# Chunk attention and a MISH feed-forward on one core: order of sums' parts, divisions ahead of conversions, weights kept from slot 4, k loaded apart, last weight sum in another buffer

## The chip, the cores and the metric

The kernel runs on one core of a Trainium2 chip. The metric is the time of one execution on the device in microseconds; the median of several runs is compared. The engines are named as in the profile: PE multiplies matrices, DVE, ACT and POOL work elementwise, SP issues nearly all transfers, which 16 DMA engines carry out.

## The reference

Attention inside chunks of 64 tokens gives 4608 tokens of 512 values; a feed-forward with the MISH function follows. All is float32.

```python
scores = scale * np.matmul(q_c, k_c.transpose(0, 1, 2, 4, 3))      # chunks of 64 x 64
scores = scores - np.max(scores, axis=-1, keepdims=True)
attn = np.exp(scores)
attn = attn / (np.sum(attn, axis=-1, keepdims=True) + 1e-09)
x = np.matmul(attn, v_c)                                           # 4608 x 512 after reordering
h = x @ w_in                                                       # 512 x 2048
sp = np.where(h > 20.0, h, np.log1p(np.exp(np.minimum(h, 20.0))))
out = (h * np.tanh(sp)) @ w_out                                    # 2048 x 512
```

## The kernel before

**Split operands.** PE multiplies in a short float format, so every float32 operand is kept as a high part (a conversion, on ACT) and a low part (operand minus high part, on DVE or POOL), and each product is three matmuls: low by high, high by high, high by low. Names with `_hi` and `_lo` make these parts.

**Order.** The whole program is written in the order in which it is to be issued (`manual_schedule`); each engine takes its own instructions in that order. SP issues transfers in order too, at most 8 of them in flight. Buffers are handed round: "turns" are rings of pieces in one tile (`st_turns`: four of 4 KB in "sums"), `Free` is a list that gives out the place that has been free longest, and the pool `at` has three 8 KB buffers for q, k, v and the like.

**Slots.** The first two blocks of 512 tokens are multiplied plainly, in 32 slots s = 0 to 31, one for each of 2 blocks and 16 slices f of the hidden width. Slot s does the up matmuls of slice s+1 (`up`, 12 matmuls into `h`), MISH and the split of its result into `g` (`g_hi`, `g_lo`), and the down matmuls of slice s-1 (`down`, 12 matmuls into `o_o`). In the first 16 slots the weights also come in: `w_load` (512 KB on SP), `w_scale` (ACT), `w_bits` (DVE), `w_hi` (ACT), `w_lo` (DVE). `keep_weights(f)` writes the split pieces that the later sets need to the chip's memory (`dwi`, `dwo`): four transfers of 256 KB for even f, two for odd f, in slot f + KEEP. The JOBS (`t_sum`, `t_diff`, `t_hi`, `t_lo`) make sums of weights and write them there too; the last one, `LAST_JOB`, is done in sets 0 and 1.

**Attention.** It is done in pairs of tiles (a pair is 256 tokens): load q and k, scores, maximum, subtract, exponential, sum and inverse (`a_inverse`), division (`a_norm`, on DVE), transposes through PE and a copy back, values. Four pairs ("quick", j = 4 to 7) are spread over slots 13 to 29: their scores fall in slots 14, 18, 22, 26, their divisions and transposes in 16, 20, 24, 28. Ten more pairs are planned in the sets by `plan_pair(j, then)`, where `then` is the step of the exponential; `on_pe` places a pair's matmuls.

**Sets.** The other 28 tiles go through a scheme of seven products for four, in sets z of 14 steps, 84 matmuls each in the steady part. Even steps hold a group of up matmuls (`s_up`, into `al`, `b` or `g`), odd steps a group of down matmuls (`s_down`, into `d`) that belongs to earlier sets. `plan_set` places the work of a set: copies of partial results out of PE's banks (`s_copy`: "p1", "u2", "p5"), additions (`s_c`), MISH (`s_mish`), sums of results ("T1" to "T4", `s_t`), and the two parts of each operand of the down matmuls (`s_hi`, `s_lo`; POOL does the low parts of 22, T2 and T3 and the sums T2 and T3). `s_out` adds `d` to "sums" on DVE, or copies it there on ACT the first time. `ring_load` and `wo_load` bring the weights of the sets back (1 MB and 512 KB each). Two slots' down matmuls and the last stores (`store`) fall into the first sets; `when(z, step, ...)` adds work to a step.

Of the kernel before, what the change touches and what calls it, by code (L numbers as in the profile page):

```python
# [18 lines left out]
P = 128  # L19
# [6 lines left out]
def kernel(  # L26
# [196 lines left out]
    def w(step, n):  # L223
        if n < len(order):
            steps[step](*order[n])
# [6 lines left out]
    def load_qk(j, qk=None, ts=(BOTH,), queues=(nc.sync, nc.sync)):  # L232
        if qk is None:
            qk = [at.tile([P, 2, H, CHUNK], F32, name=f"{n}_{j}", tag="A") for n in "qk"]
        for t in ts:
            for x, src, queue in zip(qk, (q, k), queues):
                queue.dma_start(
                    out=x[:, t], in_=src[2 * j : 2 * j + 2][t].rearrange("t p h c -> p t h c")
                )
        st[j] = {"q": qk[0], "k": qk[1]}  # L240
# [64 lines left out]
    def a_inverse(j, t=BOTH):  # L305
        p = st[j]["p"][:, t].rearrange("p t g c k -> p (t g) c k")
        r = small(j, "r", t)
        nc.vector.tensor_reduce(out=r.rearrange("p c n -> p n c"), in_=p, op=ALU.add, axis=AX.X)  # L308
        nc.vector.tensor_scalar(out=r, in0=r, scalar1=1e-9, scalar2=None, op0=ALU.add)
        nc.vector.reciprocal(out=r, in_=r)  # L310

    def a_norm(j, t=BOTH, engine=nc.vector):
        p = st[j]["p"][:, t].rearrange("p t g c k -> p c (t g) k")
        r = st[j]["r", t.start]
        engine.tensor_tensor(
            out=p, in0=p, in1=r.unsqueeze(3).broadcast_to([P, 2, r.shape[2], CHUNK]), op=ALU.mult
        )
# [297 lines left out]
    def t_hi(m, s):  # L615
        d = tw[m, s]
        for i in range(2):
            if (m, s) == LAST_JOB:
                d["s", i] = at.tile([P, 2, 2, 2 * P], F32R, name=f"s_last{i}", tag="A")
            else:  # L620
                d["s", i] = st_turns.next([2, 2, 2 * P], F32R)
            nc.scalar.copy(out=d["s", i][:, :, 0], in_=d["t", i])

    def t_lo(m, s):
# [173 lines left out]
    def s_up(z, i):  # L798
# [26 lines left out]
        [("xo", 49 * KB + i * UNIT) for i in range(4)]  # L825
        + [("u", i * UNIT) for i in range(9)]
        + [("yr", i * UNIT) for i in range(4)]
        + [("g", i * UNIT) for i in range(4)]
        + [("u", i * UNIT) for i in range(9, 18)]
    )  # L830

    def x1_open():
# [160 lines left out]
        JOBS[NF - 2 + n] = ("io"[n % 2], n // 2)  # L993

    N = NB * NF
    KEEP = 11

    def slot(s):
        a = plan.get(s, {})
        e = quick.get(s, {})  # L1000
        n = 2 * s + 3
        behind = JOBS.get(s - 1)

        if 1 <= s and s + 1 < N:
            up(s + 1, last="w")
        if "v" in e:
            a_values(e["v"])
        if a.get("t", 0) > PAIRS:
            a_transpose(a["t"])
        if "v" in a:  # L1010
            a_values(a["v"])
        if 1 <= s < N - 1:
            down(s - 1)
        if a.get("t", 0) == PAIRS:
            a_transpose(PAIRS)
        if "s" in a:
            a_scores(a["s"])
        if "s" in e:
            a_scores(e["s"])

        if NF <= s < N:
            g_hi(s)
            g_lo(s)
        if a.get("load", 0) > PAIRS:
            load_qk(a["load"])
        if "load" in e and s != NF + 1:
            load_qk(e["load"])
        w("load", n + 4)
        w("hi", n)
        w("scale", n + 2)  # L1030
        w("bits", n + 1)
        w("lo", n)
        if "max" in a:
            a_max(a["max"])
        if "max" in e:
            a_max(e["max"])
            a_sub(e["max"])
            load_v(e["max"])
        if "norm" in e:
            a_inverse(e["norm"])  # L1040
            a_norm(e["norm"])
            a_transpose(e["norm"])
        if a.get("norm", 0) > PAIRS:
            a_norm(a["norm"])
        if plan.get(s - 1, {}).get("norm", 0) == PAIRS:
            a_norm(PAIRS)
        if a.get("t", 0) > PAIRS:
            a_copy(a["t"])
        if "exp" in a:
            a_exp(a["exp"])  # L1050
        w("load", n + 5)
        if "x" in a:
            a_hi(a["x"])
        if s < NF:
            g_hi(s)
            g_lo(s)
        if s + 1 < N:
            mish(s + 1)
        if "max" in e:
            a_exp(e["max"])  # L1060
        w("hi", n + 1)
        w("scale", n + 3)
        w("bits", n + 2)
        w("lo", n + 1)
        if "max" in a:
            a_sub(a["max"])
        if a.get("exp", 0) > PAIRS:
            a_inverse(a["exp"])
        if a.get("norm", 0) == PAIRS:
            a_inverse(PAIRS)  # L1070
        if a.get("t", 0) == PAIRS:
            a_copy(PAIRS)
        if "x" in a:
            a_lo(a["x"])
        if "v" in e:
            a_x(e["v"], 0)
            a_x(e["v"], 1)
        if "norm" in e:
            a_copy(e["norm"])
        if "max" in a:  # L1080
            load_v(a["max"])
        if 0 <= s - KEEP < NF:
            keep_weights(s - KEEP)
        if behind:
            t_hi(*behind)
        if s in JOBS:
            t_sum(*JOBS[s])
        if behind:
            t_lo(*behind)
        if s in JOBS:  # L1090
            t_diff(*JOBS[s])
        if s == NF:
            load_qk(quick[s + 1]["load"])
        if s == NF:
            x_open()
        if s >= 1 and s % NF == 0:
            store(s // NF - 1)
# [3 lines left out]
    def when(z, i, *ops):  # L1101
        due.setdefault((z, i), []).extend(ops)
# [4 lines left out]
    def plan_set(z):  # L1107

        b, s = divmod(z, NS)

        def at_(m, *ops):
            when(*divmod(STEPS * z + m, STEPS), *ops)

        at_(0, lambda: s_copy(z, "p1", ("a", z)))
        at_(2, lambda: s_c(z, 11), lambda: s_mish(z, 11))
        at_(3, lambda: s_hi(z, 11))
        at_(4, lambda: s_copy(z, "u2", ("a", z)))
        at_(5, lambda: s_raw(z), lambda: s_lo(z, 11))
        at_(6, lambda: s_copy(z, "p5", "g"))
        at_(8, lambda: s_c(z, 22), lambda: s_mish(z, 22))  # L1120
        at_(9, lambda: s_hi(z, 22))
        at_(10, lambda: s_c(z, 12), lambda: s_mish(z, 12), lambda: s_lo(z, 22))
        at_(11, lambda: s_t(z, "T1"), lambda: s_t(z, "T3"))
        at_(12, lambda: s_mish(z, 21), lambda: s_hi(z, 21), lambda: s_hi(z, "T1"), lambda: s_hi(z, "T3"))
        at_(13, lambda: s_t(z, "T2"), lambda: s_lo(z, 21), lambda: s_lo(z, "T1"), lambda: s_lo(z, "T3"))
        at_(15, lambda: s_t(z, "T4"), lambda: s_hi(z, "T2"), lambda: s_lo(z, "T2"))
        at_(17, lambda: s_hi(z, "T4"), lambda: s_lo(z, "T4"))
        if s == NS - 1 and b + 1 < NSB:
            plan_x(z, b + 1)

# [11 lines left out]
    def plan_pair(j, then):  # L1142

        start = then - 5

        def at_(n, *ops):
            when(*divmod(n, STEPS), *ops)

        def on_pe(n, op):
            pe.setdefault(divmod(n, STEPS), []).append(op)  # L1150

        at_(start - 7, lambda: p_load(j))
        on_pe(start, lambda: p_scores(j))
        at_(then + 4, lambda: load_v(j))
        for t in range(2):
            at_(start + 1 + 2 * t, lambda t=t: p_max(j, t))
            at_(start + 2 + 2 * t, lambda t=t: p_sub(j, t))
            at_(then, lambda t=t: p_exp(j, t))
            at_(then + 3 + t, lambda t=t: p_sum(j, t))
            at_(then + 6 + 2 * t, lambda t=t: p_norm(j, t))  # L1160
            at_(then + 11, lambda t=t: p_copy(j, t))
            at_(then + 15, lambda t=t: a_x(j, t))
        on_pe(then + 10, lambda: p_transpose(j))
        on_pe(then + 14, lambda: p_values(j))

    ZN = NSB * NS
# [19 lines left out]
    with tc.manual_schedule():  # L1186
# [23 lines left out]
            when(0, i + 1, lambda m=m: x_lo(0, m))  # L1210
        for at_step, i, ts in (
            ((0, 1), N - 2, (0, 1)),
            ((0, 5), N - 2, (2, 3)),
            ((0, 9), N - 1, (0, 1)),
            ((1, 3), N - 1, (2, 3)),
        ):
            pe[at_step] = [lambda i=i, ts=ts: down(i, ts)]
            if i == N - 1:
                when(*at_step, lambda ts=ts: store(NB - 1, ts))
        when(0, 11, *(lambda n=n: wo_load(n) for n in range(4)))  # L1220
        slot(N - 1)
        y_open()
        banks_a.close()
# [2 lines left out]
            places[n] = ps_b.tile([P, DM], F32, name=n, tag=n)  # L1226
        for j, then in zip(range(AHEAD[-1] + 1, NPAIR), EXPS):
            plan_pair(j, then)
        for m, step in (5, t_sum), (6, t_diff), (22, t_hi), (25, t_lo):
            when(*divmod(m, STEPS), lambda step=step: step(*LAST_JOB))  # L1230
        for z in 2, 17:
            when(z, 2, x_late)
# [51 lines left out]
```

## Time and profile before

| | |
|---|---|
| median of 3 runs | 820.83 us (820.49 to 822.52) |
| profiled execution | 819.81 us, its span 818.0 us |
| busy: PE / DVE / ACT / POOL | 98% / 73% / 60% / 34% of the span |
| DMA | 202.33 MB, mean 247 GB/s |
| chain that ended last | PE 75%, DVE 11%, DMA 5%, ACT 5% |

The span is what the profiler saw of the instructions; the execution's time has some 1.8 us around it. Matmuls overlap, so a busy PE isn't a PE at its peak. In rows of a timeline the first number is the start, the second how long the group took; a bracket gives the engine's idle time just before and what ended it. The slots run to 218.5 us, the sets from there.

### The profile page before, as it was taken

The page shows a single profiled execution, that of the slowest core. Times are in us where ns is not written, and L with a number is a line of the kernel's source. Part 1 is how long each engine was busy: PE and PEld are TensorE (multiplying, and loading weights), DVE is VectorE, ACT ScalarE, POOL GpSimd, SP SyncE. Part 2 cuts the span into 40 slices and gives each one's busy share as a digit, 9 for nine tenths or more (in the row PEclk, how much of TensorE's full clock was granted, in tenths as well). Part 3 has the DMA queues.
Part 4 walks back from the last instruction along what each step waited for, and adds up shares of the span by engine and source line. Part 5 has one row for each costly group of instructions (what it writes and reads, how often), then busy time and mean ns, then how long its engine had stood idle before and what let it go on. Part 6 is the DMA issues. An engine that isn't in the chain of part 4 may idle for free.

```text
span 818.0 us, 15365 instructions
## 1 busy us (share of the span) xinstructions
PE 799.5 (98%) x5974; PEld 706.9 (86%) x5974; DVE 593.2 (73%) x929; ACT 489.2 (60%) x867; POOL 274.9 (34%) x239
## 2 busy tenths in 40 slices
PE   8999999999999999999999999999999999999996
PEld 7778887778888998888899999889999999999996
DVE  6898887778865586799657668986575888455566
ACT  5988864655667564665666556557564564644440
POOL 2100025556354332432233235333232444323340
PEclk9999999999999999999999999999999999999999
DMA  8756778999787876576986666788766667866547
GB/s 309 236 177 231 211 257 279 356 369 353 262 301 290 284 245 201 197 266 228 299 302 231 223 206 222 247 293 268 258 232 206 206 206 244 280 220 220 182 129 167
DMA packets 84553, 202.33 MB, mean 247 GB/s; under 512 B 13569, under 2 KB 36609, under 8 KB 77313
## 3 DMA queue, kind: packets, MB, share of 16 engines
q1 hardware_dynamic: 80480, 199.91, 72.7%
q10 hardware_dynamic: 4000, 1.44, 0.8%
q8 instruction: 47, 0.77, 0.4%
q14 instruction: 26, 0.20, 0.1%
HBM read 162.53 MB, written 38.80 MB: 246 GB/s over the span
## 4 chain that ended last, share of the span: by engine, by line
PE 75%; DVE 11%; DMA 5%; ACT 5%; issue 2%; SPq 1%; POOL 0%; ACTq 0%; POOLq 0%
PE d L927 30%; PE al L809 17%; PE g L809 9%; PE o_o L416 5%; PE h L381 4%; PE b L809 4%; PE av L255 2%; PE s L255 2%; DMA k<-in_k 1%; DVE sums L955 1%; DMA dwi<-sums 1%; DVE sums L958 1%; DMA ring<-dwi 1%; PE pt L719 1%; DVE r L308 1%
## 5 line engine op out<-in xcount | busy, mean ns | idle before, releaser
L927 PE MATMUL d<-u,wo 128*128 128x448 f32 x800 | 207.3, 367 | 1.2 <-DVE u L887 0.9
L955 DVE TENSOR_TENSOR sums<-d,sums 128x448 f32<-128x448 f32 x192 | 119.3, 621 | 96.1 <-PE d L927 95.2
L809 PE MATMUL al<-xo,ring 128*128 128x448 f32 x768 | 177.3, 367 | 0.8 <-ACT y L853 0.8
L927 PEld LDWEIGHTS d<-u,wo 128*128 128x128 f32 x800 | 149.5, 188 | 14.5 <-DVE sums L955 1.4
L809 PEld LDWEIGHTS al<-xo,ring 128*128 128x128 f32 x768 | 143.4, 188 | 13.9 <-ACT y L853 2.0
L809 PE MATMUL g<-xo,ring 128*128 128x448 f32 x384 | 88.7, 366 | 0.0
L809 PEld LDWEIGHTS g<-xo,ring 128*128 128x128 f32 x384 | 71.7, 188 | 5.8
L927 PE MATMUL d<-g,wo 128*128 128x448 f32 x194 | 57.2, 365 | 0.0
L927 PE MATMUL d<-yr,wo 128*128 128x448 f32 x184 | 56.2, 369 | 0.0
L877 ACT ACTIVATE y<-y 128x448 f32<-128x448 f32 x26 | 15.0, 578 | 62.6 <-DVE y L863 62.6
L877 ACT ACTIVATE b<-b 128x448 f32<-128x448 f32 x32 | 16.9, 529 | 59.4 <-DVE b L863 59.3
L927 PE MATMUL d<-xo,wo 128*128 128x448 f32 x166 | 51.3, 368 | 0.0
L887 POOL TENSOR_TENSOR u<-y,u 128x448 fp32r<-128x448 f32 x20 | 24.3, 1216 | 78.4 <-ACT u L881 78.4
L909 POOL TENSOR_TENSOR z<-y,z 128x448 f32<-128x448 f32 x27 | 32.7, 1210 | 44.3 <-DVE y L909 36.7
L809 PE MATMUL b<-xo,ring 128*128 128x448 f32 x192 | 44.7, 368 | 0.0
L610 POOL TENSOR_TENSOR c<-c 128x256 f32<-128x256 f32 x12 | 10.3, 865 | 97.9 <-DVE c L578 96.0
L887 POOL TENSOR_TENSOR g<-y,yr 128x448 fp32r<-128x448 f32 x10 | 11.6, 1158 | 94.0 <-ACT yr L881 94.0
L381 PE MATMUL h<-x,xo 128*128 128x512 f32 x168 | 41.2, 394 | 0.0
L416 PE MATMUL o_o<-xo,g 128*128 128x512 f32 x168 | 41.0, 393 | 0.0
L927 PEld LDWEIGHTS d<-g,wo 128*128 128x128 f32 x194 | 36.4, 188 | 2.9
L809 PEld LDWEIGHTS b<-xo,ring 128*128 128x128 f32 x192 | 35.7, 188 | 3.1
L927 PEld LDWEIGHTS d<-yr,wo 128*128 128x128 f32 x184 | 34.5, 188 | 3.7 <-DVE sums L955 0.6
(226 smaller groups left out, 1633.6 us busy)
## 6 DMA issues: line engine op xcount, KB each, us to landing
ring<-dwi SPq DMA_DIRECT2D x56, 1024.0 KB, 7.1
wo<-dwo SPq DMA_DIRECT2D x112, 512.0 KB, 3.9
sums<-in_w_in SPq DMA_DIRECT2D x16, 512.0 KB, 4.6
sums<-in_w_out SPq DMA_DIRECT2D x16, 512.0 KB, 4.1
q<-in_q SPq DMA_DIRECT2D x16, 512.0 KB, 7.0
k<-in_k SPq DMA_DIRECT2D x16, 512.0 KB, 6.9
v<-in_v SPq DMA_DIRECT2D x16, 512.0 KB, 6.5
dwo<-sums SPq DMA_DIRECT2D x14, 512.0 KB, 5.6
```

Of the source, the lines that this page charges most:

```text
L255: nc.tensor.matmul(o[h * CHUNK : (h + 1) * CHUNK, c, t - ts.start, g], lhsT=l[rows, t, 2 * g + h], rhs=r[rows, t, 2 * g + h], start=True, ...
L308: nc.vector.tensor_reduce(out=r.rearrange("p c n -> p n c"), in_=p, op=ALU.add, axis=AX.X)
L381: nc.tensor.matmul(h[:, cols], lhsT=wi(f, w_, kt), rhs=x[:, kt, cols], start=(n == 0), stop=(n == 3 * NK - 1),)
L416: nc.tensor.matmul(acc[t], lhsT=g[:, sl], rhs=w_part(f, w_), start=(f == 0 and n == 0), stop=(f == NF - 1 and n == 2),)
L610: nc.gpsimd.tensor_tensor(out=o, in0=a, in1=b, op=op)
L719: nc.tensor.transpose(out=d["pt"][:, t, g], in_=d["p", t][:, g].rearrange("p c k -> p (c k)"), identity=ident,)
L809: nc.tensor.matmul(o[:, :HALF], lhsT=w_[:, wn, kt * P : (kt + 1) * P], rhs=x[:, xn, kt], start=(n == 0 and k < 3), stop=(n == 5), skip_gro ...
L877: nc.scalar.activation(out=take(z, 12) if n == 12 else i, in_=i, func=AF.Mish)
L887: engine.tensor_tensor(out=u[1][1], in0=source(z, n), in1=raw(u[0][1]), op=ALU.subtract)
L909: engine.tensor_tensor(out=o, in0=l, in1=r, op=ALU.subtract)
L927: nc.tensor.matmul(o[:, :HALF], lhsT=wos[(len(DOWN) * y + kk) % 4][:, i, part, h * P : (h + 1) * P], rhs=x, start=(m == 0 and k in (5, 2, 1)),
L955: nc.vector.tensor_tensor(out=o, in0=i, in1=o, op=ALU.add)
```

## The change

1. KEEP goes from 11 to 4: the pieces of weights are written in slots 4 to 19, where it was 11 to 26.
2. In the slots of the quick pairs the inverse and the division stand ahead of the conversions `g_hi` and `g_lo`, of the loads and of the weights' steps.
3. The last two quick pairs' k is loaded at the end of the slot before, ahead of the writes of that slot, and q at the start of the slot, each with an instruction of its own (`e_load`).
4. The last job's high and low parts go to two turns of "sums" instead of two buffers of `at`, at steps 20 and 23 instead of 22 and 25.
5. `tiles` gives out its places in another order at first.
6. In `plan_set` the high part of T1 comes ahead of that of 21, and the parts of T2, T3 and T4 move two to three steps back.
7. In `plan_pair` q and k are loaded two steps earlier, the divisions stand one step earlier, the transposes and copies one later.
8. The last slots' down matmuls and stores are spread further over sets 0 and 1; the first four loads of `wo` move from step 11 to step 1 of set 0.

```diff
@@ t_hi
-            if (m, s) == LAST_JOB:
-                d["s", i] = at.tile([P, 2, 2, 2 * P], F32R, name=f"s_last{i}", tag="A")
-            else:
-                d["s", i] = st_turns.next([2, 2, 2 * P], F32R)
+            d["s", i] = st_turns.next([2, 2, 2 * P], F32R)
@@ tiles
+        + [("u", i * UNIT) for i in range(9, 13)]
         + [("g", i * UNIT) for i in range(4)]
-        + [("u", i * UNIT) for i in range(9, 18)]
+        + [("u", i * UNIT) for i in range(13, 18)]
@@
-    KEEP = 11
+    KEEP = 4
+
+    def e_load(j, n):
+        if j not in st:
+            st[j] = {
+                m: at.tile([P, 2, H, CHUNK], F32, name=f"{m}_{j}", tag="A") for m in "qk"
+            }
+        src = {"q": q, "k": k}[n][2 * j : 2 * j + 2]
+        nc.sync.dma_start(out=st[j][n], in_=src.rearrange("t p h c -> p t h c"))
@@ slot
+        if "norm" in e:
+            a_inverse(e["norm"])
+            a_norm(e["norm"])
         if NF <= s < N:
             g_hi(s)
             g_lo(s)
         if a.get("load", 0) > PAIRS:
             load_qk(a["load"])
-        if "load" in e and s != NF + 1:
+        if "load" in e and s < NF:
             load_qk(e["load"])
+        if "load" in e and s > NF + 1:
+            e_load(e["load"], "q")
         w("load", n + 4)
...
         if "norm" in e:
-            a_inverse(e["norm"])
-            a_norm(e["norm"])
             a_transpose(e["norm"])
...
+        later = quick.get(s + 1, {})
+        if "load" in later and s > NF:
+            e_load(later["load"], "k")
         if 0 <= s - KEEP < NF:
             keep_weights(s - KEEP)
@@ plan_set
-        at_(12, lambda: s_mish(z, 21), lambda: s_hi(z, 21), lambda: s_hi(z, "T1"), lambda: s_hi(z, "T3"))
...
+        at_(12, lambda: s_mish(z, 21), lambda: s_hi(z, "T1"), lambda: s_hi(z, 21))
...
+        at_(17, lambda: s_hi(z, "T2"), lambda: s_t(z, "T4"), lambda: s_lo(z, "T2"))
+        at_(19, lambda: s_hi(z, "T4"))
+        at_(20, lambda: s_lo(z, "T4"))
@@ plan_pair
-        at_(start - 7, lambda: p_load(j))
+        at_(8 if then == EXPS[0] else start - 9, lambda: p_load(j))
...
-            at_(then + 6 + 2 * t, lambda t=t: p_norm(j, t))
-            at_(then + 11, lambda t=t: p_copy(j, t))
+            at_(then + 5 + 2 * t, lambda t=t: p_norm(j, t))
+            at_(then + 12, lambda t=t: p_copy(j, t))
...
-        on_pe(then + 10, lambda: p_transpose(j))
+        on_pe(then + 11, lambda: p_transpose(j))
@@ the last slots' down matmuls and stores
             ((0, 1), N - 2, (0, 1)),
-            ((0, 5), N - 2, (2, 3)),
-            ((0, 9), N - 1, (0, 1)),
-            ((1, 3), N - 1, (2, 3)),
+            ((0, 7), N - 2, (2, 3)),
+            ((1, 5), N - 1, (0, 1)),
+            ((1, 13), N - 1, (2, 3)),
...
-        when(0, 11, *(lambda n=n: wo_load(n) for n in range(4)))
+        when(0, 1, *(lambda n=n: wo_load(n) for n in range(4)))
@@
-        for m, step in (5, t_sum), (6, t_diff), (22, t_hi), (25, t_lo):
+        for m, step in (5, t_sum), (6, t_diff), (20, t_hi), (23, t_lo):
```

SP's transfers from slot 4 on, before. `sums<-in_w_in` and `sums<-in_w_out` are the weight loads, `q` and `k` those of an attention pair; the number after a name tells one use of a tile from the next.

```order
L162 DMA sums<-in_w_in 128x1024
L162 DMA sums<-in_w_out 128x1024
L162 DMA sums<-in_w_in 128x1024
L237 DMA q_793<-in_q 128x2x512
L237 DMA k_794<-in_k 128x2x512
L162 DMA sums<-in_w_out 128x1024
```

The same place after:

```order
L162 DMA sums<-in_w_in 128x1024
L559 DMA dwi_100<-ring 128x2x256 x2
L561 DMA dwo_114<-ring 128x2x256 x2
L162 DMA sums<-in_w_out 128x1024
L162 DMA sums<-in_w_in 128x1024
L559 DMA dwi_101<-ring 128x2x256
L561 DMA dwo_114<-ring 128x2x256
L237 DMA q_799<-in_q 128x2x512
L237 DMA k_800<-in_k 128x2x512
L162 DMA sums<-in_w_out 128x1024
```

The writes of pieces (`dwi`, `dwo`) now stand between the loads of the weights.

DVE in slot 20, before. `z<-xo` and `c<-xo` begin the next job, L403 is `g_lo`, L308 to L315 are inverse and division.

```order
L628 TENSOR_TENSOR sums<-z,sums 128x2x256 x2
L403 TENSOR_TENSOR g<-h_1568,g 128x512
L308 TENSOR_REDUCE r_0_1647<-p_1597 128x8x2
L309 TENSOR_SCALAR r_0_1647<-r_0_1647 128x16
L310 RECIPROCAL r_0_1647<-r_0_1647 128x16
L315 TENSOR_TENSOR p_1597<-p_1597,r_0_1647 128x2x8x64
L578 TENSOR_TENSOR z<-xo 128x512
```

After, where `t_lo` is line 625:

```order
L625 TENSOR_TENSOR sums<-z,sums 128x2x256 x2
L308 TENSOR_REDUCE r_0_1665<-p_1619 128x8x2
L309 TENSOR_SCALAR r_0_1665<-r_0_1665 128x16
L310 RECIPROCAL r_0_1665<-r_0_1665 128x16
L315 TENSOR_TENSOR p_1619<-p_1619,r_0_1665 128x2x8x64
L403 TENSOR_TENSOR g<-h_1590,g 128x512
L578 TENSOR_TENSOR z<-xo 128x512
```

The subtraction for g's low part went behind the division; `t_lo` of the job stayed ahead of both.

ACT around step 20 (step 6 of set 1), before. L436 copies a store out of its bank, L853 is `s_copy` (`y<-al` is "u2", `y<-g` is "p5"), L622 is `t_hi` of the last job.

```order
L436 COPY sums<-o_o_1458 128x512
L881 CAST u<-y 128x448
L881 CAST yr<-b 128x448
L853 COPY y<-al_2445 128x448
L892 COPY y<-b 128x448
L853 COPY y<-g 128x448
L622 CAST s_last_2503<-c 128x2x256
L622 CAST s_last_2505<-c 128x2x256
L877 ACTIVATE z<-z 128x448
```

After, with the lines 851, 879, 890, 619 and 875 for 853, 881, 892, 622 and 877:

```order
L879 CAST u<-b 128x448
L851 COPY y<-al_2435 128x448
L436 COPY sums<-o_o_1479 128x512
L879 CAST yr<-y 128x448
L890 COPY y<-b 128x448
L619 CAST sums<-c 128x2x256 x2
L851 COPY y<-g 128x448
L875 ACTIVATE z<-z 128x448
```

The copy of `al` now stands ahead of the store's copy, the two casts of the last job ahead of the copy of `g`.

More of the change, by code (lines that the diff above doesn't have):

```diff
@@ L1123, in plan_set @@
         at_(11, lambda: s_t(z, "T1"), lambda: s_t(z, "T3"))
-        at_(12, lambda: s_mish(z, 21), lambda: s_hi(z, 21), lambda: s_hi(z, "T1"), lambda: s_hi(z, "T3"))
-        at_(13, lambda: s_t(z, "T2"), lambda: s_lo(z, 21), lambda: s_lo(z, "T1"), lambda: s_lo(z, "T3"))
-        at_(15, lambda: s_t(z, "T4"), lambda: s_hi(z, "T2"), lambda: s_lo(z, "T2"))
-        at_(17, lambda: s_hi(z, "T4"), lambda: s_lo(z, "T4"))
+        at_(12, lambda: s_mish(z, 21), lambda: s_hi(z, "T1"), lambda: s_hi(z, 21))
+        at_(13, lambda: s_t(z, "T2"), lambda: s_lo(z, "T1"), lambda: s_lo(z, 21))
+        at_(15, lambda: s_hi(z, "T3"), lambda: s_lo(z, "T3"))
+        at_(17, lambda: s_hi(z, "T2"), lambda: s_t(z, "T4"), lambda: s_lo(z, "T2"))
+        at_(19, lambda: s_hi(z, "T4"))
+        at_(20, lambda: s_lo(z, "T4"))
         if s == NS - 1 and b + 1 < NSB:
```

## The prediction

> **What bounds the kernel.** I read the busy shares and the chain first, then the costliest groups:
>
> ```profile
> span 818.0 us, 15365 instructions
> PE   799.5 (98%) x5974; PEld 706.9 (86%) x5974; DVE 593.2 (73%) x929; ACT 489.2 (60%) x867; POOL 274.9 (34%) x239
> PE 75%; DVE 11%; DMA 5%; ACT 5%; issue 2%; SPq 1%; POOL 0%; ACTq 0%; POOLq 0%
> L955 DVE TENSOR_TENSOR sums<-d,sums 128x448 f32<-128x448 f32 x192 | 119.3, 621 | 96.1 <-PE d L927 95.2
> ```
>
> PE is the bound: it is busy 98% of the span and carries 75% of the chain. The additions of partial results on DVE wait for PE's `d` (95.2 of 96.1 us of idle time), not PE for them. The edit alters no matmul, so all it can win is time in which PE stands still or runs late. Next I took stretches, for PE's true pace and for the load on the DMA engines:
>
> ```profile
> core 0: us, PE busy (x) PEld busy (x) DVE busy (x) ACT busy (x) POOL busy (x), PEclk, DMA share, GB/s
> 45.00:95.00 50.00, 48.80 (x333) 39.37 (x332) 43.96 (x68) 43.20 (x74) 0.00 (x0) 1.00 0.64 209
> 95.00:107.00 12.00, 12.00 (x117) 9.67 (x116) 10.88 (x17) 9.54 (x17) 0.00 (x0) 1.00 0.94 268
> 107.00:113.00 6.00, 6.00 (x28) 4.87 (x26) 4.81 (x7) 3.86 (x7) 0.00 (x0) 1.00 0.96 332
> 152.00:160.00 8.00, 7.45 (x95) 6.20 (x96) 5.65 (x9) 5.33 (x9) 4.61 (x6) 1.00 1.07 390
> 700.00:720.00 20.00, 20.00 (x101) 18.53 (x100) 9.03 (x15) 9.72 (x21) 6.01 (x5) 1.00 0.83 283
> ```
>
> The clock is 1.00 in each. In 700:720, 101 matmuls start in 20.0 us: 0.198 us from start to start, while one is shown as 0.367 us long (the waits below follow such matmuls). Busy time therefore hides the overlap, and an idle gap of g costs g + 0.367 - 0.198 = g + 0.17; I use 0.16. A set has 84 matmuls (1344 of L809 and as many of L927 over 32 sets), so 16.6 us, or 1.19 us for each of its 14 steps.
>
> Last, PE's timeline at each gap. The bracket is the idle time and what ended it:
>
> ```profile
> 125.97 1.06 PE L324 MATMUL pt<-ident,p 128*128 128x128 f32 x8 [0.30 <-DVE p L315]
> 152.55 1.06 PE L324 MATMUL pt<-ident,p 128*128 128x128 f32 x8 [1.09 <-DVE p L315]
> 166.97 1.16 PE L255 MATMUL s<-k,q 64*64 64x64 f32 x64 [1.12 <-DMA k<-in_k]
> 179.53 1.06 PE L324 MATMUL pt<-ident,p 128*128 128x128 f32 x8 [0.30 <-DVE p L315]
> 205.33 1.07 PE L324 MATMUL pt<-ident,p 128*128 128x128 f32 x8 [0.30 <-DVE p L315]
> 238.32 0.88 PE L809 MATMUL al<-xo,ring 128*128 128x448 f32 x3 [0.82 <-ACT y L853]
> 246.14 0.47 PE L927 MATMUL d<-u,wo 128*128 128x448 f32 x1 [0.87 <-DVE u L887]
> 310.50 1.16 PE L255 MATMUL s<-k,q 64*64 64x64 f32 x64 [0.31 <-DMA k<-in_k]
> 328.44 1.49 PE L927 MATMUL d<-u,wo 128*128 128x448 f32 x6 [0.36 <-DVE sums L955]
> 388.99 0.66 PE L719 MATMUL pt<-ident,c 128*128 128x128 f32 x4 [0.83 <-DVE c L709]
> 540.80 0.66 PE L719 MATMUL pt<-ident,c 128*128 128x128 f32 x4 [0.83 <-DVE c L709]
> ```
>
> Their idle time is 7.13 us; with 11 x 0.16 they cost 8.9 us. That is nearly all there is to win, 1% of the span.
>
> **Part by part.**
>
> *Divisions ahead of conversions* (slots 16, 20, 24, 28). DVE's queue in slot 20:
>
> ```profile
> 148.84 0.68 DVE L403 TENSOR_TENSOR g<-h,g 128x512 fp32r<-128x512 f32 x1
> 149.44 1.21 DVE L308 TENSOR_REDUCE r<-p 128x16 f32<-128x1024 f32 x1
> 151.18 1.22 DVE L315 TENSOR_TENSOR p<-p,r 128x1024 f32<-128x1024 f32 x1
> ```
>
> The division ends at 152.40 and the transposes start at 152.55. With g_lo (L403) behind it, it ends 149.44 - 148.84 = 0.60 earlier. In slots 16, 24 and 28 the wait is 0.30, less than 0.60, and goes: 3 x 0.46 = 1.38. In slot 20 0.60 of 1.25 goes. Together 1.98. The low part of g now ends some 2.9 us later; the next slot's down matmuls read it, behind twelve up matmuls, so it costs nothing.
>
> *Loads of q and k apart, weights kept from slot 4: the late k.* The row 166.97 waits for this load:
>
> ```profile
> k<-in_k SPq DMA_DIRECT2D x1, 512.0 KB, 6.3
> ```
>
> It was issued at 160.56, behind keep writes, in a stretch at 390 GB/s (152:160). Afterwards slots 20 and later hold no keep writes, and k's issue waits only for slot 20's transposes, near 153. Even 6.3 us from there land it 7 us ahead of the scores: 1.12 + 0.16 = 1.28 gained. q waits for the values matmuls, near 157; at 7 us it lands near 164, in time by 2.
>
> *What the early writes cost.* Slots 4 to 11 take over eight f of writes: 4 x 1.049 + 4 x 0.524 = 6.29 MB. The stretch 45:95 moved 209 GB/s x 50 = 10.45 MB, so it must now move 16.74 MB, or 335 GB/s: above the 332 of 107:113, below the 390 of 152:160. Two weight loads show what an issue behind writes means, the first alone, the second behind four writes:
>
> ```profile
> sums<-in_w_in SPq DMA_DIRECT2D x1, 512.0 KB, 3.4
> sums<-in_w_out SPq DMA_DIRECT2D x1, 512.0 KB, 6.5
> 95.78 1.22 DVE L315 TENSOR_TENSOR p<-p,r 128x1024 f32<-128x1024 f32 x1
> 97.18 1.04 PE L324 MATMUL pt<-ident,p 128*128 128x128 f32 x8
> ```
>
> A load is up to 3.1 us later. Everything on SP stands behind the writes, and behind a late load stand ACT's scaling, DVE's bits and PE's up matmuls. The last two rows show a place in slot 12 with no slack: DVE ends at 97.00, PE starts at 97.18 without a wait. Bounds: 0 (the loads have that much slack) and 2.0 (PE is that much late once; a delay of PE moves the later deadlines too). I take 1.0, the middle, since the rate asked lies between the two rows.
>
> By the Trainium skill's "Perfetto Trace Analysis", section Roofline, 358 GB/s is a core's share while its neighbour is active, and one core alone may pull about 120% of it. The 390 GB/s row agrees that one core passes 358. By that rule this cost is 0 and the sum is 1.0 better.
>
> *The last job of weight sums, stores and `d`* (sets 0 to 2). Before, ACT's copy of `al` stands behind a store's copy and two casts (PE's 238.32), and two subtractions of t_lo hold DVE until `u` is late (246.14):
>
> ```profile
> 237.71 0.56 ACT L853 COPY y<-al 128x448 f32<-128x448 f32 x1
> 238.56 0.58 ACT L853 COPY y<-g 128x448 f32<-128x448 f32 x1
> 238.98 1.19 ACT L622 CAST s_last<-c 128x512 fp32r<-128x512 f32 x2
> 241.60 2.24 DVE L628 TENSOR_TENSOR s_last<-c,s_last 128x512 fp32r<-128x512 f32 x2
> 241.83 1.47 POOL L887 TENSOR_TENSOR g<-z,yr 128x448 fp32r<-128x448 f32 x1 [4.92 <-ACT yr L881]
> 245.01 1.07 DVE L887 TENSOR_TENSOR u<-y,g 128x448 fp32r<-128x448 f32 x1
> out<-sums SPq DMA_DIRECT2D x4, 128.0 KB, 6.8
> ```
>
> Both go: 0.98 + 1.03 = 2.0. New: the two casts (1.19) stand ahead of the copy of `g`, so PE's next sum in that bank starts about 0.65 late, 0.8 with the restart. And the first `d` takes the banks of the last store, whose DVE copy follows ACT's copy behind the casts: 0 to 0.9, I take 0.6. Net 0.6; bounds 0 and 2.0. The first copy of `d` to "sums" must also wait for the stores' writes; PE needs that bank again 18 matmuls (3.6 us) later, and the writes took 6.8 us here: that is a rival below.
>
> By the Trainium skill's "SBUF — State Buffer", section Who interferes with whom, a DVE instruction with two SBUF inputs and a GpSimd one that reads SBUF shut each other out. The trace agrees: 2.24 us for two subtractions beside POOL's 1.47. The pair still stands beside a POOL subtraction afterwards; if it takes 2.24 again, the first `d` is 0.9 late instead of 0.6, and the net is 0.3.
>
> *Attention pairs in the sets.* q and k go two steps (2.4 us) earlier, ahead of the ring load they followed:
>
> ```profile
> ring<-dwi SPq DMA_DIRECT2D x1, 1024.0 KB, 6.6
> q<-in_q SPq DMA_DIRECT2D x1, 512.0 KB, 9.4
> k<-in_k SPq DMA_DIRECT2D x1, 512.0 KB, 10.2
> ```
>
> The wait at 310.50 (0.47) goes; the ring load then stands behind 1 MB, but its weights are used at least a set later. The division goes one step earlier and the transposes one later, 2.4 us of distance against waits of 0.83: 388.99 and 540.80 go, 2 x 0.99 = 1.98. 328.44 goes since T4's subtraction (about 0.62, the length of L955) leaves the place ahead of that addition: 0.52. Together 2.97. T2, T3 and T4's later parts cost nothing: the first of these operands, T2, is read by PE 16 steps (19 us) after its new step 17.
>
> *Small ones.* The order of `tiles` changes names only. Some copies and transposes of the sets start 0.1 to 0.2 us late before; I set them off against new waits of that size.
>
> *Sum*: 1.98 + 1.28 - 1.0 + 0.6 + 2.97 = 5.83 us. The profiled execution took 819.81 (818.0 and 1.8 around it), 1.02 less than the median: 814.0 for such an execution, **815.0** as a median.
>
> **Rivals.**
> 1. *All waits go and nothing new comes*: 8.9 less the 0.65 that slot 20 keeps is 8.25 gained: 812.6; with the small late starts of the sets, some 0.9 more, 811.7. For it: the 390 GB/s row. Against it: the new order on ACT, which can be read from the program.
> 2. *Stores late for the first `d`*: ACT waits 6.8 us for the writes where PE has 3.6: 3.2 lost, 815.0 + 3.2 = 818.2. For it: the 6.8 row. Against it: the stores now come apart from each other, and the bank's users are spread.
> 3. *The waits only move on*: k's, the divisions' and the last job's gaps return as waits of the same size on weights: 820.5. Against it: the rows show idle queues behind most gaps.
> 4. *Slower: the DMA engines bound slots 4 to 11.* At the 268 GB/s of 95:107, the one stretch that mixes these loads with these writes, 16.74 MB take 62.5 us instead of 50: 12.5 lost, 815.0 - 1.0 + 12.5 = 826.5. The kernel comes out slower below 16.74 / (50 + 6.8 + 2.5) = 282 GB/s. Against it: that stretch begins with 2 us without a transfer and the next one, with the same writes, moves 332.
>
> **Numbers.** My forecast 0.56, rivals 0.16, 0.12, 0.09, 0.07 in their order. A measurement of this kernel can hardly tell less than 0.3% (2.5 us) from no change. My forecast's own range is 812.5 to 818; faster than 818.4 are it, the first rival and half the second: 0.78. Slower than 823.3 is the last: 0.07. The remaining 0.15 lies between. The range 811.2 to 820.2 takes in the forecast, the first two rivals and part of the third.
>
> **What the profile after would show.** Right: the transposes of slots 16, 24, 28 and the pairs without a bracket, slot 20's with about 0.5; no wait for k; the early stretch near 330 GB/s, with up to 2 us of new gaps. Wrong: PE gaps in 45:95 ended by ACT or DVE on weights (too little taken for the writes); a gap of over 1 us at the first or second `d` (rival 2); waits on `p`, `u` or `sums` inside many sets, which I cost at nothing.

## The result and the profile after

The changed kernel takes 815.68 us (median of 6 runs, 813.05 to 818.46) against 820.77 before (6 runs, 819.58 to 822.52): a ratio of 0.9932, 95% interval 0.9908 to 0.9957. Forecast were 815.0 and a range of 811.2 to 820.2. Two later series of the same kernel gave 0.9929 (0.9914 to 0.9943) and 0.9945 (0.9927 to 0.9963). One execution below, of 1314 us, had a granted clock of 0.557, where all others had 0.996 to 0.999; it stands in no ratio. The profiled execution happened to be the longest of the first six, 818.46 us; its page:

```profile
span 816.7 us, 15329 instructions
PE 800.3 (98%) x5974; PEld 707.4 (87%) x5974; DVE 596.1 (73%) x929; ACT 485.2 (59%) x867; POOL 270.7 (33%) x239
PE 83%; DVE 7%; ACT 4%; DMA 3%; issue 1%; SPq 0%; POOL 0%; ACTq 0%; POOLq 0%; DVEq 0%
```

PE now carries 83% of the chain, where it was 75%. All eleven gaps of the prediction's list are gone from PE's timeline, slot 20's too. In their place stand these:

```profile
92.84 0.50 PE L416 MATMUL o_o<-xo,g 128*128 128x512 f32 x1 [0.70 <-DVE g L403]
99.98 0.41 PE L324 MATMUL pt<-ident,p 128*128 128x128 f32 x2 [1.38 <-DVE p L315]
231.76 0.47 PE L806 MATMUL al<-xo,ring 128*128 128x448 f32 x1 [0.22 <-ACT sums L851]
237.83 0.69 PE L806 MATMUL g<-xo,ring 128*128 128x448 f32 x2 [0.80 <-ACT y L851]
250.88 0.67 PE L925 MATMUL d<-xo,wo 128*128 128x448 f32 x2 [1.66 <-ACT sums L951]
```

That is 4.76 us idle, with restarts 5.6, against 8.9 that went: 3.3 us won at these places in this trace. The stretches show where the transfers went, from slots 20 and later to the early ones:

```profile
45.00:95.00 50.00, 47.92 (x328) 38.19 (x327) 41.31 (x63) 40.45 (x69) 0.00 (x0) 1.00 0.93 302
140.00:200.00 60.00, 60.00 (x565) 49.11 (x564) 48.21 (x63) 35.36 (x54) 36.44 (x38) 1.00 0.83 289
```

Before, 45:95 had 209 GB/s and 140:200 had 361; there PE now works all 60 us, where it worked 57.49.

**The early gaps.** Three rows of ACT's timeline show their source:

```profile
70.43 0.66 ACT L169 ACTIVATE c<-sums 128x512 f32<-128x512 f32 x1 [3.81 <-DMA sums<-in_w_out]
87.92 0.68 ACT L169 ACTIVATE c<-sums 128x512 f32<-128x512 f32 x1 [0.95 <-DMA sums<-in_w_out]
91.45 0.60 ACT L398 CAST g<-z 128x512 fp32r<-128x512 f32 x1
```

ACT stands still until a weight load lands that went out among the writes. Behind its scaling stand an exponential with its table load and the cast of g (91.45); DVE's subtraction waits for that cast, and PE for it at 92.84. The division, further back on DVE, ends at 99.84, and PE waits again.

**The stores.** The first copy of `d` waits on ACT for the last stores, as the second rival had it:

```profile
236.17 1.18 ACT L619 CAST sums<-c 128x512 fp32r<-128x512 f32 x2
237.21 0.57 ACT L851 COPY y<-g 128x448 f32<-128x448 f32 x1
250.29 0.53 ACT L951 COPY sums<-d 128x448 f32<-128x448 f32 x1 [4.23 <-DMA out<-sums]
out<-sums SPq DMA_DIRECT2D x4, 128.0 KB, 5.8
```

The four writes of the last two stores, issued from 243.0 on, took 5.8 us to land, behind a ring load and two writes of the last job. The first two rows are the casts ahead of the copy of `g`, which make the 0.80 at 237.83.

### The profile page after: what moved, and what is told of

Its sections match the earlier page's. It is cut to its first block, busy times and chain, and to the rows that moved or that the text cites. A ratio compares the mean times of both kernels' runs of the same rounds, so it can differ in the third digit from the quotient of the medians.

```text
span 816.7 us, 15329 instructions
## 1 busy us (share of the span) xinstructions
PE 800.3 (98%) x5974; PEld 707.4 (87%) x5974; DVE 596.1 (73%) x929; ACT 485.2 (59%) x867; POOL 270.7 (33%) x239
## 4 chain that ended last, share of the span: by engine, by line
PE 83%; DVE 7%; ACT 4%; DMA 3%; issue 1%; SPq 0%; POOL 0%; ACTq 0%; POOLq 0%; DVEq 0%
PE d L925 32%; PE al L806 18%; PE g L806 9%; PE o_o L416 7%; PE h L381 6%; PE b L806 5%; PE s L255 2%; PE av L255 2%; PE pt L716 1%; DVE c L191 1%; DMA sums<-in_w_out 1%; ACT c L169 1%; DMA dwo<-xo 1%; DVE sums L953 1%; DVE c L192 1%
## 5 line engine op out<-in xcount | busy, mean ns | idle before, releaser
L806 PE MATMUL al<-xo,ring 128*128 128x448 f32 x768 | 178.3, 367 | 0.2 <-ACT sums L851 0.2
L806 PEld LDWEIGHTS al<-xo,ring 128*128 128x128 f32 x768 | 143.4, 188 | 13.5 <-ACT sums L851 0.6
L806 PE MATMUL g<-xo,ring 128*128 128x448 f32 x384 | 89.0, 367 | 0.8 <-ACT y L851 0.8
L806 PEld LDWEIGHTS g<-xo,ring 128*128 128x128 f32 x384 | 71.9, 188 | 7.4 <-ACT y L851 1.2
L925 PE MATMUL d<-xo,wo 128*128 128x448 f32 x182 | 55.8, 369 | 1.7 <-ACT sums L951 1.7
L925 PE MATMUL d<-g,wo 128*128 128x448 f32 x174 | 52.6, 367 | 0.2 <-DVE sums L953 0.2
L806 PE MATMUL b<-xo,ring 128*128 128x448 f32 x192 | 44.8, 368 | 0.0
L907 POOL TENSOR_TENSOR z<-y,z 128x448 f32<-128x448 f32 x24 | 28.5, 1189 | 38.0 <-DVE y L907 24.2
L875 ACT ACTIVATE z<-g 128x448 f32<-128x448 f32 x32 | 17.5, 546 | 38.8 <-DVE g L861 23.3
L875 ACT ACTIVATE y<-y 128x448 f32<-128x448 f32 x22 | 12.7, 578 | 46.5 <-DVE y L861 46.4
L885 POOL TENSOR_TENSOR u<-y,yr 128x448 fp32r<-128x448 f32 x12 | 13.9, 1155 | 79.4 <-ACT yr L879 79.4
L806 PEld LDWEIGHTS b<-xo,ring 128*128 128x128 f32 x192 | 35.7, 188 | 3.3
L925 PEld LDWEIGHTS d<-xo,wo 128*128 128x128 f32 x182 | 34.0, 188 | 5.1 <-ACT sums L951 2.0
```

Source lines behind the costliest of these rows:

```text
L806: nc.tensor.matmul(o[:, :HALF], lhsT=w_[:, wn, kt * P : (kt + 1) * P], rhs=x[:, xn, kt], start=(n == 0 and k < 3), stop=(n == 5), skip_gro ...
L875: nc.scalar.activation(out=take(z, 12) if n == 12 else i, in_=i, func=AF.Mish)
L885: engine.tensor_tensor(out=u[1][1], in0=source(z, n), in1=raw(u[0][1]), op=ALU.subtract)
L907: engine.tensor_tensor(out=o, in0=l, in1=r, op=ALU.subtract)
L925: nc.tensor.matmul(o[:, :HALF], lhsT=wos[(len(DOWN) * y + kk) % 4][:, i, part, h * P : (h + 1) * P], rhs=x, start=(m == 0 and k in (5, 2, 1)),
```

## The experiments

**The changed kernel again, twice** (no edit; the second time beside the last three versions).

> The changed kernel once more, for a second trace and its spread. Theory: the six executions of the result lie 5.4 us apart because the new gaps wait for transfers (weights behind writes in slots 9 to 13, the stores ahead of the first copy of `d`), whose landing times differ between executions. It expects the same four gaps on PE (0.70 at 92.8, 1.38 at 100.0, 0.80 at 237.8, 1.66 at 250.9) of which those two groups differ by more than 0.3 us from the first trace, the 0.80 not; time 813 to 818. Rival: the spread comes from the clock (0.4 us more for every 20 us from 640 us on in the first trace); then the gaps are as before within 0.1 us and the steady part of the sets runs at another pace.

> The changed kernel a third time, beside the next three on one chip. Theory (waits on transfers differ between executions): 813 to 816, gaps of 2.0 to 2.6 us with restarts near 92 and 99, 0.96 at 238, 0.7 to 1.9 at 250, and at the scores of slot 22 (near 167) anything from 0 to 1.8. Rival: the same gaps as in the second trace within 0.1 us.

Measured: 814.83 us (814.33 to 815.81; span of the profile 813.2) and 816.19 (813.54 to 817.67; span 814.0). The early gaps came back in both (0.43 and 1.38 in the first), the one at 238 too. Two others vary: the wait for the stores at 250, and one for q in slot 22 that is absent from the trace above. The rows are from the first series, but for the third, which is from the second:

```profile
250.70 0.47 PE L925 MATMUL d<-xo,wo 128*128 128x448 f32 x1 [0.64 <-ACT sums L951]
167.77 0.45 PE L255 MATMUL s<-k,q 64*64 64x64 f32 x14 [1.62 <-DMA q<-in_q]
168.78 0.41 PE L255 MATMUL s<-k,q 64*64 64x64 f32 x13 [0.70 <-DMA q<-in_q]
q<-in_q SPq DMA_DIRECT2D x1, 512.0 KB, 9.6
```

So q of slot 22 is late in two traces of three: issued at 158.1 it took 9.6 us in the first series; in the trace above it was issued at 158.7, took 7.4 and was in time. The early gaps differ by 0.27 at most, where I expected over 0.3. The rival holds in part: the first trace has a slower pace at its end, though not at another granted clock. In 640:780, where no gap stands, before, the first trace and the repeat read:

```profile
640.00:780.00 140.00, 140.00 (x691) 129.02 (x690) 91.93 (x143) 71.51 (x139) 55.34 (x44) 1.00 0.67 223
640.00:780.00 140.00, 140.00 (x680) 127.18 (x679) 91.07 (x140) 69.49 (x137) 48.36 (x42) 1.00 0.66 217
640.00:780.00 140.00, 140.00 (x692) 129.62 (x691) 92.52 (x143) 70.80 (x140) 48.88 (x41) 1.00 0.67 220
```

680 matmuls instead of 692 at 0.203 us each are 2.4 us of the 3.5 us between the two spans. Both causes thus part these traces; how far each makes the spread of the other executions isn't shown.

**KEEP back at 11.**

```diff
-    KEEP = 4
+    KEEP = 11
```

> The changed kernel with KEEP back at 11, all else as changed. Theory: the writes beside the weight loads cost the gaps at 92.8 and 100.0, 2.1 us idle and 2.4 with the restarts; they go, PE has no new gap in 45:107, and the load on the DMA engines there falls from 302 to about 209 GB/s. Slots 20 to 26 get the writes back; since k is issued ahead of them it is in time all the same, or late by under 0.5 us. Time: 1.5 to 2.5 us less than the changed kernel. Rival (the writes in slots 20 to 26 were what made k late, the order of issue alone doesn't help): a gap of about 1 us before the scores of slot 22 or 26, time the same as the changed kernel.

Measured: 815.15 us, a ratio of 0.9928 (0.9912 to 0.9945); the changed kernel beside it had 814.83 and 0.9929. That is no gain, where 1.5 to 2.5 us were expected:

```profile
97.69 0.52 PE L324 MATMUL pt<-ident,p 128*128 128x128 f32 x3 [0.40 <-DVE p L315]
152.59 0.63 PE L324 MATMUL pt<-ident,p 128*128 128x128 f32 x4 [0.93 <-DVE p L315]
168.46 0.75 PE L255 MATMUL s<-k,q 64*64 64x64 f32 x36 [2.58 <-DMA dwo<-xo]
```

The early gaps go but for 0.40, and slots 20 and 22 take back 3.5 us. The time is the rival's, but its cause isn't: k, issued at 156.4 ahead of the writes, landed at 163.2, 5 us before the scores. It was q, issued at 160.3 behind them, that landed at 168.2, just before the scores (the profile names another transfer that ended there).

**KEEP 4 alone, in the kernel before.**

```diff
-    KEEP = 11
+    KEEP = 4
```

> The kernel before with one part of the change, KEEP 4. Theory: it costs 2.0 to 2.6 us by gaps near 92 and 99 (as the changed kernel shows), which go back nowhere, and gains 1.3 at most by k's being in time in slot 22 (k and q are still issued together, after slot 21's start near 160, and without writes in front): time 0.5 to 1.5 us more than before, 821.5 to 822.5. Rival: the early gaps shift PE later, so that the waits of slots 16 to 22 shrink by as much, since these wait for chains that do not shift; time equal to before or up to 1 us less.

Measured: 820.11 against 819.87, a ratio of 1.0006 (0.9997 to 1.0014). The time is the rival's. Two rows of this kernel's PE, then k's issue for slot 22, in the kernel before and in this one:

```profile
98.71 0.52 PE L324 MATMUL pt<-ident,p 128*128 128x128 f32 x3 [1.37 <-DVE p L315]
153.20 1.07 PE L324 MATMUL pt<-ident,p 128*128 128x128 f32 x8 [0.30 <-DVE p L315]
160.56 0.54 SPq L237 DMA_DIRECT2D k<-in_k  x1
158.53 1.17 SPq L237 DMA_DIRECT2D k<-in_k  x1
```

The early gaps (0.53 at 91.6 and this one) cost 2.2 us. Slot 20 gives 0.79 of it back, since PE comes there later: its gap falls from 1.09 to 0.30. The gap for k, 1.28 with the restart, is gone for the theory's reason and not the rival's: without slot 20's writes of pieces in front k went out 2.0 us earlier and landed at 165.2 instead of 166.9, in time. So some 2.0 us come back, and nothing is won.

**Division first, alone.** In the kernel before, `a_inverse` and `a_norm` of the quick pairs go ahead of `g_hi` and `g_lo`.

```diff
+        if "norm" in e:
+            a_inverse(e["norm"])
+            a_norm(e["norm"])
         if NF <= s < N:
             g_hi(s)
             g_lo(s)
```

> The kernel before with one part of the change, the division ahead of the conversions in the quick pairs' slots. Theory: the gaps ahead of the transposes of slots 16, 24 and 28 (0.30 each) go and that of slot 20 falls from 1.09 to about 0.5; with the restarts 2.0 us less: 818.8. Rival: slot 20's gap goes wholly, as it did in the changed kernel, so that the division alone had made it; 2.6 us less. Rival on the other side: the down matmuls of the next slot wait for the later low part of g; new gaps with the releaser L403, no gain.

Measured: 819.99 against 820.99, a ratio of 0.9991 (0.9976 to 1.0007): no gain clear of the noise, where 2.0 us were expected.

```profile
151.40 0.84 PE L324 MATMUL pt<-ident,p 128*128 128x128 f32 x6 [0.47 <-DVE p L315]
166.71 0.47 PE L255 MATMUL s<-k,q 64*64 64x64 f32 x17 [2.02 <-DMA k<-in_k]
```

Slots 16, 24 and 28 lost their gaps and slot 20 kept 0.47, as worked out (0.49). But PE came to the scores of slot 22 earlier while k hardly did (it landed at 166.6, before at 166.9): that gap grew from 1.12 to 2.02. No wait on L403 came up.

**The part in plan_pair alone**, in the kernel before; the first pair's load stays where it was.

```diff
-        at_(start - 7, lambda: p_load(j))
+        at_(start - 7 if then == EXPS[0] else start - 9, lambda: p_load(j))
...
-            at_(then + 6 + 2 * t, lambda t=t: p_norm(j, t))
+            at_(then + 5 + 2 * t, lambda t=t: p_norm(j, t))
...
-        on_pe(then + 10, lambda: p_transpose(j))
+        on_pe(then + 11, lambda: p_transpose(j))
```

> The kernel before with one part of the change, the one in plan_pair (q and k two steps earlier from the second pair on, divisions one step earlier, transposes and copies one later). Theory: the gaps ahead of the second transposes near 389 and 541 (0.83 each) go and no wait for k is left near 310: with the restarts 2.0 to 2.5 us less than before, 818.5 to 819.0. The late k of slot 22 and the gaps of slots 16 to 28 stay. Rival: the ring loads, now behind q and k, come late instead, with gaps ahead of L809 and no gain.

Measured: 817.76 against 819.87, 0.9980 (0.9967 to 0.9994). No gap is left near 310, 389 or 541, and no ring load comes late: 2.1 us by the medians, 1.6 by the ratio, about as expected. The transposes near 389 now start without a wait:

```profile
388.19 1.04 PE L719 MATMUL pt<-ident,c 128*128 128x128 f32 x8
```

The gap near 310 is also missing from the traces of KEEP 4 alone and of the division alone, so this run doesn't show that its removal is this part's work. Of the three parts that ran alone, it is the only one that clearly shortens the run.

**Last job, last stores and wo loads as before**, in the changed kernel.

```diff
-            ((1, 5), N - 1, (0, 1)),
-            ((1, 13), N - 1, (2, 3)),
+            ((0, 9), N - 1, (0, 1)),
+            ((1, 3), N - 1, (2, 3)),
...
-        for m, step in (5, t_sum), (6, t_diff), (20, t_hi), (23, t_lo):
+        for m, step in (5, t_sum), (6, t_diff), (22, t_hi), (25, t_lo):
```

> The changed kernel with the last job's buffers and steps, the last stores and the first loads of wo as before (the first pair's q and k at their old step too). Theory: this part moved the gaps rather than removed them; 0.80 at 237.8 and 1.66 at 250.9 go, 0.82 and 0.87 near 238 and 246 come back; time within 1 us of the changed kernel (0.8 us less by the two sums 2.0 against 2.8). Rival: it was worth more than its gaps show, for instance by the transfers around it, and the time rises by over 1.5 us.

Measured: 814.64 against the changed kernel's 814.83. No worth of this part can be told from these times. The gaps at 237.8 and 250.9 went, these came:

```profile
243.99 0.47 PE L928 MATMUL d<-u,wo 128*128 128x448 f32 x1 [0.79 <-DVE u L888]
251.81 0.59 PE L255 MATMUL s<-k,q 64*64 64x64 f32 x25 [0.86 <-DMA k<-in_k]
```

The 0.82 near 238 did not return, against my expectation; so this part alone isn't what had removed it.

**plan_set as before**, in the changed kernel, once with the old order of `tiles` and once with the new.

```diff
-        at_(12, lambda: s_mish(z, 21), lambda: s_hi(z, "T1"), lambda: s_hi(z, 21))
+        at_(12, lambda: s_mish(z, 21), lambda: s_hi(z, 21), lambda: s_hi(z, "T1"), lambda: s_hi(z, "T3"))
...
-        at_(19, lambda: s_hi(z, "T4"))
-        at_(20, lambda: s_lo(z, "T4"))
+        at_(17, lambda: s_hi(z, "T4"), lambda: s_lo(z, "T4"))
```

> The changed kernel with the parts in plan_set and the order of `tiles` as before. Theory: these two are worth the one gap near 328 (0.36 idle, 0.52 with the restart) and nothing in any other set: that gap comes back, the time is 0.3 to 0.7 us more than the changed kernel's 814.8 to 815.7. Rival: they also take small waits out of the sets, and PE's excess between 400 and 780 us grows by over 1 us.

> The changed kernel with the part in plan_set alone as before; the order of `tiles` stays changed. Theory: the gap near 328 (0.36 to 0.44) comes back; the one at 231 grows from 0.2 to about 1.1, since the conversions and subtractions of T1, T2 and T3 stand ahead of the copies there; the pace of the later sets is the same. 1.0 to 2.0 us more than the changed kernel. Rival: the gap at 231 came from the old order of `tiles`, not from plan_set; then it stays at 0.2 and the time is 0.5 us more.

Measured: 0.9970 (0.9958 to 0.9982) with the old order, 0.9964 (0.9950 to 0.9978) with the new; the changed kernel beside the latter 0.9945. By medians the second is 1.5 us slower than the changed kernel, as expected, but the intervals overlap. The first had 816.99 us, over the 0.3 to 0.7 us that were expected. In the first of the two the sets write into places of `g` that the last slot's late down matmuls have still to read, so part of the values change, and PE has a gap of its own (its row first, the other two from the second kernel):

```profile
241.63 0.73 PE L416 MATMUL o_o<-u,g 128*128 128x512 f32 x2 [1.11 <-ACT g L878]
232.47 0.86 PE L806 MATMUL al<-xo,ring 128*128 128x448 f32 x3 [1.10 <-ACT sums L851]
328.29 0.90 PE L925 MATMUL d<-u,wo 128*128 128x448 f32 x3 [0.43 <-DVE sums L953]
```

With the new order the gap at 231 grows from 0.22 to 1.10 and 328 comes back, as expected; from 400 us on the sets run alike. So `plan_set`'s part matters at 231, where ACT also copies stores, and between 280 and 400 us, and the order of `tiles` is what makes room for the late down matmuls.

**A further version.** The writes follow a table, the last job's casts stand behind the copy of `g`, and the last two stores go through a buffer of `at` (these have 4 KB each, not 8 as said above).

```diff
+    KEEPS = {5: (0,), 6: (1,), 7: (2,), 9: (3,), 10: (4,), 11: (5,), 12: (6, 7), 13: (8, 9),
+             14: (10, 11), 15: (12, 13), 16: (14,), 17: (15,)}
...
+        late = at.tile([P, 2, DM], F32, name="o_late", tag="A") if b and ts == (2, 3) else None
...
-        for m, step in (5, t_sum), (6, t_diff), (20, t_hi), (23, t_lo):
+        for m, step in (5, t_sum), (6, t_diff), (21, t_hi), (23, t_lo):
```

> The changed kernel with three more edits. The pieces of weights are written by a table, none in slot 4 and 8, one f each in 5 to 7 and 9 to 11, two f each in slots 12 to 15, one in 16 and 17. The casts of the last job stand one step later (21), behind the copy of `g`. The last two stores go through a buffer of `at`, so that the first copy of `d` to the sums needn't wait for their writes. Theory: the gaps at 92 and 99 shrink to under 0.5 together, q and k of slot 22 are in time, the gaps at 238 (0.80) and 250.8 (0.64 to 1.66) go: 3 to 5 us less than the changed kernel, 810.5 to 812. Rival: the waits of the early slots only move, since DVE and ACT are late there for themselves (86 to 89% busy); the gap at 99 stays over 1 us, time 813 to 814.

Measured: 812.68 against 819.87, 0.9922 (0.9909 to 0.9935). The profile's span, 809.7, is 3.5 and 4.3 us less than the two repeats' spans, but it is that of the fastest of five executions; by the ratios the gain over the changed kernel is 0.6 and 1.9 us, within the noise, where 3 to 5 us were expected. The gaps at 238, 251 and 167 are gone. The early ones only moved, as the rival said of the one at 99:

```profile
73.99 0.73 PE L416 MATMUL o_o<-xo,g 128*128 128x512 f32 x2 [1.01 <-DVE g L403]
99.11 0.63 PE L324 MATMUL pt<-ident,p 128*128 128x128 f32 x4 [1.35 <-DVE p L315]
```

**Two other tables** in that version: four f beside the loads, then none.

```diff
+    KEEPS = {4: (0,), 5: (1,), 8: (2,), 9: (3,), 12: (4, 5), 13: (6, 7), 14: (8, 9),
+             15: (10, 11), 16: (12,), 17: (13,), 18: (14,), 19: (15,)}
```

> As the version with a table of writes, but with only four f beside the loads: one in slots 4, 5, 8 and 9, two in 12 to 15, one in 16 to 19. Theory: the gaps at 74 and 99 come from single weight loads that land 2 us and more later behind writes, so that ACT waits for them and casts g late; with no writes in slots 6, 7, 10 and 11 the two cost under 1.2 us together (2.7 in the version before), q and k of slot 22 stay in time: 810.5 to 812.5. Rival: it's enough that any one load is late, and the gap at 99 stays at 1.5 us; no gain over that version.

```diff
+    KEEPS = {12 + n: (2 * n, 2 * n + 1) for n in range(4)}
+    KEEPS.update({16 + n: (8 + n,) for n in range(8)})
```

> The same with no writes beside the loads at all: two f in slots 12 to 15, one in 16 to 23. Theory: no gap in 56:96, at most the 0.57 near 98 that KEEP 11 showed; but the writes in slots 20 to 23 put the q or k of slot 22 at risk, 0 to 2.5 us. 811 to 813.5. Rival: the traffic of slots 12 to 15 makes new gaps of over 1 us near 113 to 135 (scores and transposes of slots 14 and 16).

Measured: 0.9916 (0.9895 to 0.9936) and 0.9927 (0.9909 to 0.9945); the first had five runs from 811.02 to 815.37 us, besides the one of 1314. The medians, 813.84 us of these five and 814.13, lie above both expected ranges. One row each:

```profile
97.31 0.95 PE L324 MATMUL pt<-ident,p 128*128 128x128 f32 x7 [1.10 <-DVE p L315]
166.20 0.99 PE L255 MATMUL s<-k,q 64*64 64x64 f32 x53 [2.33 <-DMA dwi<-u]
```

With four f the early cost is one gap, 1.10; with none PE has no new early gap of over 0.15, which shows that the writes beside the loads make these gaps, but slot 22 waits 2.33. No gap of the rival's kind came up at 113 to 135. The times of the three versions can't be told apart, nor each of them surely from the changed kernel; that they lack the gaps at 238 and 251 the traces show.

## Why the prediction was right, point by point

The total fits (5.1 us by the medians, 5.83 forecast), but with luck: terms off in both directions cancel. PE does the same matmuls in both kernels, so the time between two of them shows what a stretch gained. I take the first up matmul of the slots (at 18.0 us), that of set 4 and that of set 20. These two start so before (L809) and in the first trace after (L806):

```profile
279.50 0.47 PE L809 MATMUL al<-xo,ring 128*128 128x448 f32 x1
584.95 0.36 PE L809 MATMUL al<-xo,ring 128*128 128x448 f32 x1
280.00 0.47 PE L806 MATMUL al<-xo,ring 128*128 128x448 f32 x1
580.50 0.37 PE L806 MATMUL al<-xo,ring 128*128 128x448 f32 x1
```

| stretch | before | after, three traces | gained | forecast |
|---|---|---|---|---|
| slots to set 4 | 261.5 us | 262.0, 262.4, 261.5 | -0.9 to 0.0 | 2.86 |
| set 4 to set 20 | 305.4 us | 300.5, 300.2, 300.2 | 5.0 to 5.2 | 2.97 |

The first stretch is known to about 1 us only: it took 262.7 with `plan_pair` alone, which changes little there. So the four terms ahead of set 4 (1.98 + 1.28 - 1.0 + 0.6) came to little or nothing, and `plan_pair` and `plan_set` gave nearly all of the gain. The second stretch took 302.0 with `plan_pair` alone and 301.9 with `plan_set` as before, so each of the two has a share. It took 304.8 in the traces of KEEP 4 alone and of the division alone, which change nothing there, so 4.3 is the more careful figure. Even that is 1.3 more than forecast. The step that was too small is the one on late starts of 0.1 to 0.2 us in the sets, "I set them off against new waits of that size": they went, and no new ones came. Two of the forecast's signs of being wrong showed up besides: a gap in 45:95 ended by DVE (0.70 at 92.84), and one of 1.66 at an early `d`.

- *Division first*: 1.98 forecast. At its own places it is exact (0.47 left in slot 20, 0.49 forecast). What I left out is that PE, once earlier, waits longer for the next thing that does not get earlier: k, with 0.90 of it.
- *The late k*: 1.28 forecast; with q's new waits of 0, 1.78 and 0.86 (restarts included) in three traces it is 0.4 on average. The step that failed is "k's issue waits only for slot 20's transposes, near 153": it went out at 155.8 to 158.0, since the writes of slots 19 and 20 stand ahead of it on SP. It still landed in time; q, for which I gave 7 us and two to spare, took 7.4 to 9.6 and did not in two traces.
- *Early writes*: 1.0 taken, 0 to 2.0 as bounds; the gaps cost 2.1 to 2.4. Loads took up to 8.9 us, not 6.5, in a stretch of 302 GB/s: the row of one load behind four writes was too mild for a queue that stays full. But KEEP 4 alone costs nothing: slot 20 gives 0.79 back, and the earlier k 1.28. By the 120% of the Trainium skill's "Perfetto Trace Analysis", section Roofline, there would have been no cost. The gaps came at 302 GB/s, below even its 358, with the DMA engines busy for 0.93 of the stretch; no run here tells whether the place in the queue or the engines' load made the weights late.
- *Last job, stores, `d`*: 0.6 net forecast; old gaps 2.0, new ones 2.1 to 3.2, so nothing to a loss of 1.2. The casts' term was near (0.65 forecast, 0.78 to 0.80 idle measured). The first `d` was not late; instead rival 2's wait for the stores came, at 0.5 to 1.7 us. The two subtractions of the last job took 1.28 us this time, not 2.24: POOL's subtraction no longer met them, so the collision by the rule of the Trainium skill's "SBUF — State Buffer", section Who interferes with whom, did not take place, and the net of 0.3 forecast for it wasn't tested.
- *Attention pairs*: 2.97 forecast, 4.3 to 5.2 in the table; all four gaps went, and plan_pair alone gave 2.1 us of the run's time. The gap at 328 is plan_set's.
- *Slot 20's remaining 0.65* went as well, because the early gaps bring PE there later: with KEEP back at 11 a gap of 0.93 stands there.

## What to carry to other kernels

A gap is a difference between two arrivals: before you book its removal, see which arrival is tied to PE and which to a chain of transfers, for time won ahead of a late transfer is lost there again, and of time lost ahead of a late arrival a part comes back. Moving 12.6 MB of writes from one stretch to another moved the waits with them. What paid was more distance between an instruction and the one that waits for it, in stretches where the engines have room (`plan_pair`, `plan_set`). Add up small late starts too: they can weigh as much as the gaps that a timeline shows. For a load behind writes on one queue, take its time from a stretch where the queue stays full.

## What the runs showed of the hardware

In single executions PE's pace dropped by 1.7% over the last fifth (680 against 692 matmuls in 140 us) while the profile's granted clock for the stretch reads 1.00; it stood in two of the traces, the first of the changed kernel and the one with four f beside the loads; its cause is open. And the same transfer in the same place took 7.4 us in one execution and 9.6 in another.
